# A decode layer on one Trainium2 core: other rows of w_down are loaded ahead, and on other queues

## The chip, the cores and the metric

The kernel runs on one core of a Trainium2 chip. The metric is the device time of one execution in microseconds. The kernel before has a median of 226.14 us over three runs (226.1 to 226.29).

## The reference

One token with 1024 features goes through an attention and a gated feed-forward layer side by side, and both are added to the token. Everything is float32.

```python
xn = _layernorm(x)
# attention: 32 query heads, 4 key/value heads of 128, the last W = 4096 rows of the cache
q = (xn @ wq).reshape(B, Sq, 32, 128).transpose(0, 2, 1, 3)
p = softmax(einsum("bhqd,bhkd->bhqk", q, k) * 128 ** -0.5)
A = einsum("bhqk,bhkd->bhqd", p, v)... @ wo          # 4096 -> 1024
# feed-forward: 1024 -> 3584 -> 1024
B = (gelu(xn @ w_gate) * (xn @ w_up)) @ w_down
return x + A + B
```

Every weight is used once, for one token. So each of the 94 MB of weights and cache rows is read from HBM once and used a single time.

## The kernel before, in words

All weights pass through one SBUF tensor, `ring`, with 32768 floats in each of 128 partitions. `PLAN` (lines 256 to 263) lists the loads in their order: what is loaded, to which place in the ring, and after the use of which earlier load. `used(key)` issues the loads that wait for `key`. Nearly all loads are issued by SyncE, on its queue. The order is wq, the first half of the keys and values, w_gate, the second half of keys and values, w_gate, w_up, wo, and last w_down in three groups of 16, 8 and 4 tiles, `("d", 0)` to `("d", 2)`. A tile of w_down is 128 rows by 1024 columns; row 4p + t of the last group's 512 rows is in partition p of its tile t.

Each weight is multiplied by a vector. TensorE does it for half of the tiles, as four matmuls that each write one of four partition groups of PSUM (`accumulate`, line 715); VectorE does it for the others by multiplying and adding into a partial sum (`add_scaled`), which TensorE adds up at the end (`units`). The results of the four column strips lie in partitions 31, 32, 95 and 96 (`ROW`). The token itself is loaded twice: as `x_rows` for the norm, and as `x_out` in these four partitions for the last sum.

`Flow` records every instruction's reads and writes, and in a second pass it gives each instruction the semaphore waits that it needs. An instruction waits in its engine's own order; what stands behind it on the same engine waits with it.

The last group, `("d", 2)`, has four tiles, 24 to 27. In the kernel before its first two tiles come in three loads (lines 319 to 325): all 2048 columns for the partitions 0, 2, 4, ..., all 2048 for 1, 5, 9, ..., and 1280 for 3, 7, 11, .... The other 768 columns of these 32 rows, which belong to tile 25, are loaded by `load_moved` (line 335), in ten small DMAs, nine of three rows and one of five. They are issued by SyncE between wo and w_down, as `("m", 0)` of the plan, and go to a tile of their own, `moved`. The last 768 columns of tile 25's place in the ring are cleared first by GpSimd (line 321), after wo's use of that part of the ring has ended, so that the 32 rows which don't come with these loads read as zero.

```python
nc.sync.dma_start(loaded[key][0:P:2, :2 * n], both[0:P:2])
nc.sync.dma_start(loaded[key][1:P:4, :2 * n], both[1:P:4])
nc.sync.dma_start(loaded[key][3:P:4, :end], both[3:P:4, :end])
```

The factors for these rows are picked out of the hidden vector by small matmuls and copies at the end of `hidden` (lines 685 to 698) into `moved_h`; `downs` (line 734) adds the moved rows on VectorE before it comes to the w_down tiles. All other factors of w_down lie in `hz`, one column for each tile.

After the first two tiles come tile 26, and tile 27 in three column pieces. The last sum takes the left half of tile 27 first, then the right half in two steps, and four stores end the kernel.

Of the kernel before, what the change touches and what calls it, by code (L numbers as in the profile page):

```python
# [5 lines left out]
F32 = mybir.dt.float32  # L6
# [5 lines left out]
P = 128  # L12
D = 1024
# [4 lines left out]
DF = 3584  # L18
NR = 4
NJ = D // (NR * P)  # L20
NB = 512
NA = DF // NB
CO = D // 4
TD = DF // P
WIDE = 16
DOWN = (16, 8, 4)
# [5 lines left out]
GELU_C = math.sqrt(2.0 / math.pi)  # L32

ROW = (31, 32, 95, 96)
MC = 768
MOVED = ((0, 0, 0, 12, 4), (0, 1, 12, 12, 4), (1, 0, 24, 5, 1), (1, 1, 29, 3, 1))
SIZES = {"tp": NB, "acc": 2 * NB, "part": 8 * NB, "rows": 2 * NB}


# [188 lines left out]
class Pool:  # L228
# [34 lines left out]
]  # L263

# [1 line left out]
def decode_layer(nc, x, k_cache, v_cache, wq, wo, w_gate, w_up, w_down, out):  # L266
    consts = stream = work = Pool(nc.nc, "sbuf")
# [11 lines left out]
    def grouped(w, start, rows):  # L279
        return w[start:start + P * rows, :].rearrange("(p t) n -> p t n", p=P)  # L280
# [17 lines left out]
    loaded = {}  # L298

    def load(key, at):  # L300
        kind, i = key
        if kind == "m":
            load_moved()
            return
        src = source(*key)
        if kind in "kv":

            loaded[key] = dst = ring[:, at:at + RING // 4]
            if kind == "v":
                nc.sync.dma_start(dst, src)  # L310
            else:
                for odd in range(2):
                    nc.sync.dma_start(dst[odd:P:2], src[:, odd])
            return
        rows, n = src.shape[1:]
        loaded[key] = ring[:, at:at + rows * n]
        dst = loaded[key].rearrange("p (t n) -> p t n", n=n)
        pieces = PIECES[i] if kind == "d" else (0, rows)
        if key == ("d", 2):
            end = 2 * n - MC  # L320
            nc.gpsimd.memset(loaded[key][:, end:2 * n], 0.0)
            both = src[:, 0:2].rearrange("p t n -> p (t n)")
            nc.sync.dma_start(loaded[key][0:P:2, :2 * n], both[0:P:2])
            nc.sync.dma_start(loaded[key][1:P:4, :2 * n], both[1:P:4])
            nc.sync.dma_start(loaded[key][3:P:4, :end], both[3:P:4, :end])
            pieces = pieces[1:]
        for t, end in zip(pieces, pieces[1:]):
            ends = (0, n // 2, 3 * n // 4, n) if key == ("d", 2) and end == rows else (0, n)
            for cols in (slice(*cut) for cut in zip(ends, ends[1:])):
                nc.sync.dma_start(dst[:, t:end, cols], src[:, t:end, cols])  # L330

    moved = consts.tile([P, 2, MC], F32, name="moved")
    moved_h = consts.tile([P, 2], F32, name="moved_h")

    def load_moved():


        rest = w_down[DF - 4 * P:, D - MC:].rearrange("(r x) n -> x r n", x=16)[13]
        for s, a, first, count, step in MOVED:
            for j in range(step):  # L340
                to = 32 * a + j
                nc.sync.dma_start(
                    moved[to:to + 4 * (count // step):4, s], rest[first + j:first + count:step]
                )

    def used(key):

        for new, at, old in PLAN:
            if old == key:
                load(new, at)  # L350
# [3 lines left out]
    x_in = x.rearrange("a b (j p) -> (a b j) p", j=NJ)  # L354
# [1 line left out]
        nc.scalar.dma_start(x_rows[j:j + 1, :], x_in[j:j + 1, :])  # L356
    x_out = work.tile([P, CO], F32, name="x_out")
    nc.vector.memset(x_out, 0.0)
    x_in = x.rearrange("a b (h c n) -> (a b c) h n", h=2, c=4)
    for c in (0, 2):  # L360
        nc.scalar.dma_start(
            x_out[ROW[c]:ROW[c] + 2, :].rearrange("c (h n) -> c h n", h=2), x_in[c:c + 2]
        )

    ident = consts.tile([P, P], F32, name="ident")
    nc.gpsimd.memset(ident, 0.0)
    nc.gpsimd.affine_select(
        out=ident, in_=ident, compare_op=ALU.not_equal, fill=1.0, base=0,
        pattern=[[-1, P]], channel_multiplier=1,
    )  # L370
    avg = consts.tile([P, P], F32, name="avg")
    nc.vector.memset(avg, 1.0 / D)

# [4 lines left out]

    hz = consts.tile([P, TD + 1, 32], F32, name="hz")
    nc.vector.memset(hz, 0.0)  # L380
    nc.gpsimd.memset(moved, 0.0)
    nc.gpsimd.memset(moved_h, 0.0)
    oz = consts.tile([P, HQ + 1, 32], F32, name="oz")
    nc.vector.memset(oz, 0.0)
    units = consts.tile([P, 2, 32], F32, name="units")
# [62 lines left out]
    def add_scaled(total, w, factor, first):  # L448

        if first:  # L450
            nc.vector.tensor_scalar(total, w, factor, None, op0=ALU.mult)
        else:
            nc.vector.scalar_tensor_tensor(total, w, factor, total, op0=ALU.mult, op1=ALU.add)
# [210 lines left out]
    def hidden():  # L664

        h_p = small("h_p")
        kept = ((0, 16, 0, 4), (1, 8, 0, 2), (1, 4, 2, 1))
        t = at = 0  # L670
        for b, count, c, n in kept:
            k = rows[b]
            m = NB // count
            flat = copies[b][:k].rearrange("p a n -> p (a n)")
            for i in range(count):
                nc.tensor.matmul(
                    h_p[:, at + i:at + n * count:count], flat[:, i:P * count:count],
                    ident[:k, 32 * c:32 * (c + n):32], start=True, stop=True,
                )
            for own in range(n):  # L680
                r = slice(m * own, m * own + m)
                cols = slice(at + count * own, at + count * own + count)
                nc.vector.tensor_copy(hz[r, t:t + count, 31], h_p[r, cols])
            t, at = t + count, at + n * count
        k = rows[1]
        flat = copies[1][:k, 0]
        spans = []
        for s, a, first, count, step in MOVED:
            start = 16 * first + 13
            taken = flat[:, start:min(start + 80 * step, NB):4 * step]  # L690
            n = taken.shape[1]
            nc.tensor.matmul(
                h_p[32 * a:32 * a + n, at + s:at + s + 1], taken, ident[:k, 64:65],
                start=True, stop=True,
            )
            spans.append((slice(32 * a, 32 * a + n), s))
        for r, s in spans:
            nc.vector.tensor_copy(moved_h[r, s:s + 1], h_p[r, at + s:at + s + 1])


    out_p = psum.tile([P, CO], F32, name="out_p", tag="out")
# [10 lines left out]
        stores.append(len(nc.ops))  # L712
        queue.dma_start(dst[c:c + 2], rows[ROW[c]:ROW[c] + 2, :])

    def accumulate(p, z, t, w, start, stop):
        w = w.rearrange("p (h c n) -> p c h n", c=4, n=CO // 2)
        z = z.rearrange("p t m -> p (t m)")
        for c in range(4):
            at = 32 * (t + c) + 31 - ROW[c]
            nc.tensor.matmul(  # L720
                p[32 * c:32 * c + 32], z[:, at:at + 32], w[:, c], start=start, stop=stop
            )

    def outputs(i):
# [9 lines left out]
    def downs():  # L734

        tiles = [loaded["d", i][:, n * D:(n + 1) * D] for i in range(3) for n in range(DOWN[i])]
        for s in range(2):
            add_scaled(out_part[:52, D - MC:], moved[:52, s], moved_h[:52, s:s + 1], False)
        for t in KEPT:
            add_scaled(out_part, tiles[t], hz[:, t, 31:32], False)  # L740
        order = [t for t in range(DOWN[0]) if t not in KEPT]
        half = DOWN[0] + DOWN[1] // 2
        for t in [*order[:6], *range(DOWN[0], half), *order[6:], *range(half, TD - 4)]:
            accumulate(out_p, hz, t, tiles[t], False, False)
        accumulate(out_p, units, 0, out_part, False, False)
        for t in range(TD - 4, TD - 1):
            accumulate(out_p, hz, t, tiles[t], False, t == TD - 2)

        n = CO // 2
        t, wt = TD - 1, tiles[TD - 1]  # L750
        nc.vector.tensor_add(y, out_p, x_out)
        first_p = small("first_p")[:, :n]
        accumulate(first_p, hz, t, wt[:, :NB], True, True)
        nc.vector.tensor_add(y[:, :n], y[:, :n], first_p)
        store(0, 0, y[:, :n])
        store(0, 2, y[:, :n])
        last_p = psum.tile([P, 2, NB], F32, name="last_p", tag="acc")
        z = hz.rearrange("p t m -> p (t m)")
        for c in (0, 2):
            r = slice(32 * c, 32 * c + 64)  # L760
            for k in (c, c + 1):
                at = 32 * (t + k) + 31 - ROW[k]
                nc.tensor.matmul(
                    last_p[32 * k:32 * k + 32, c // 2, :n], z[:, at:at + 32],
                    wt[:, NB + n * k:NB + n * k + n], start=True, stop=True,
                )
            nc.vector.tensor_add(y_last[r], y[r, n:], last_p[r, c // 2, :n])
            store(1, c, y_last)

    used(None)  # L770
    layer_norm()
    state = None
    half = RING // 8
# [77 lines left out]
```

## Time and profile before

| | before |
|---|---|
| time, median of three runs | 226.14 us |
| span of the profiled execution, first to last instruction | 224.8 us |
| SyncE's DMA queue (q1), share of the sixteen engines' span | 97.8% |
| moved over DMA, mean | 421 GB/s |
| TensorE busy / VectorE busy | 126.0 us / 112.1 us |
| GpSimd busy | 2.8 us |
| mean granted TensorE clock | 0.795 |

The profile describes one execution. Its time as a whole is not recorded beside the span; the span is 1.3 us below the median of the runs, and that difference lies before the first and after the last instruction. The share of a DMA queue is the time that its packets took, over the span of all sixteen DMA engines. Where the queue view is asked for a short stretch, it counts the packets that start in it, with their whole time, so a share can be over 100%. The chain of waits goes back from the last instruction, at each step to what released it.

### The profile page before, as it was taken

The numbers are of one execution on the slowest core, as the hardware profiler recorded it, in microseconds if no ns is written. First come the engines' busy times: TensorE is split into PE (matmuls) and PEld (weight loads), VectorE is DVE, ScalarE is ACT, GpSimd is POOL, SyncE is SP. The second block draws the span as 40 slices with busy tenths as digits, with TensorE's granted clock in tenths as the row PEclk, the third lists the DMA queues.
The fourth block names the chain that finished last, engine by engine and source line by source line (L and its number), as shares of the span: only waits on it lengthen the run. The fifth ranks groups of instructions, "written<-read, shape, count | busy, mean of one in ns | idle before, by whom it ended". The sixth has DMA issues, their size and how long they took to land.

```text
span 224.8 us, 2511 instructions
## 1 busy us (share of the span) xinstructions
PE 126.0 (56%) x1107; PEld 65.6 (29%) x1107; DVE 112.1 (50%) x142; ACT 28.2 (13%) x54; POOL 2.8 (1%) x9
## 2 busy tenths in 40 slices
PE   0120910539899891999836751237308988900976
PEld 0010200104634731755601110001003887400442
DVE  7030920591333282336039489339708932992942
ACT  2030000002415600454400220000000000000000
POOL 3000000000000000000000000000000000010000
PEclk9999975596969999799988795557965855665699
DMA  9889889799997999999989999999989989999994
GB/s 374 374 385 548 373 373 560 338 408 464 439 490 338 429 443 452 391 488 408 472 355 449 434 449 429 490 399 420 469 385 455 467 385 461 434 397 394 426 407 172
DMA packets 3194, 94.53 MB, mean 421 GB/s; under 512 B 446, under 2 KB 718, under 8 KB 1040
## 3 DMA queue, kind: packets, MB, share of 16 engines
q1 hardware_dynamic: 3160, 94.38, 97.8%
q8 instruction: 8, 0.13, 0.2%
q14 instruction: 2, 0.02, 0.0%
q10 hardware_dynamic: 24, 0.01, 0.0%
HBM read 94.38 MB, written 0.00 MB: 420 GB/s over the span
## 4 chain that ended last, share of the span: by engine, by line
DMA 67%; DVE 20%; PE 10%; SPq 1%; ACT 1%; issue 1%; POOL 0%; DVEq 0%
DMA ring<-in_B_w_gate 26%; DMA ring<-in_A_wq 18%; DMA ring<-in_A_wo 13%; DVE part L225 13%; DMA ring<-in_B_w_down 10%; PE tp L225 6%; PE out L225 3%; DVE out_part L225 3%; DVE rows L225 2%; SPq L225 1%; PE acc L225 1%; DVE g_sb L225 1%; ACT kT L225 1%; DVE hz L225 1%; DVE kT L225 0%
## 5 line engine op out<-in xcount | busy, mean ns | idle before, releaser
L225 PE MATMUL acc<-ring,xz 128*32 128x512 f32 x176 | 32.2, 808 | 37.3 <-DMA ring<-in_A_wq 22.2
L225 DVE SCALAR_TENSOR_TENSOR part<-ring,xz,part 128x3584 f32<-128x3584 f32 (+1 forms) x9 | 37.2, 4129 | 22.0 <-DMA ring<-in_A_wq 12.5
L225 PE MATMUL tp<-ident,ring 128*128 128x128 f32 x128 | 21.0, 309 | 7.1 <-DMA ring<-in_A_k_cache 5.0
L225 PEld LDWEIGHTS acc<-ring,xz 128*32 128x32 f32 x176 | 7.2, 139 | 58.2 <-issue 26.7
L225 DVE SCALAR_TENSOR_TENSOR out_part<-ring,oz,out_part 128x1024 f32<-128x1024 f32 x16 | 20.6, 1285 | 0.6
L225 PEld LDWEIGHTS tp<-ident,ring 128*128 128x128 f32 x128 | 15.4, 154 | 16.7 <-DMA ring<-in_A_k_cache 5.9
L225 PE MATMUL out<-ring,hz 128*32 128x256 f32 x168 | 12.1, 438 | 13.5 <-DMA ring<-in_B_w_down 13.4
L225 DVE COPY kT<-tp 128x512 f32<-128x512 f32 x12 | 8.1, 690 | 19.1 <-PE tp L225 19.1
L225 PE MATMUL out<-ring,oz 128*32 128x256 f32 x120 | 12.0, 586 | 9.6 <-DMA ring<-in_A_wo 9.6
L225 ACT ACTIVATE kT<-tp 128x512 f32<-128x512 f32 x20 | 11.5, 596 | 26.6 <-PE tp L225 26.6
L225 PE MATMUL tp<-ident,kT 128*128 128x4 f32 (+4 forms) x64 | 13.4, 343 | 1.6 <-DVE hz L225 1.6
L225 PEld LDWEIGHTS tp<-ident,kT 128*128 128x128 f32 (+2 forms) x64 | 13.1, 294 | 2.2 <-DVE hz L225 1.8
L225 PE MATMUL acc<-part,units 128*32 128x512 f32 x44 | 8.1, 817 | 8.7 <-DVE part L225 8.7
L225 DVE TENSOR_SCALAR part<-ring,xz 128x3584 f32<-128x3584 f32 (+1 forms) x3 | 6.5, 2171 | 12.3 <-DMA ring<-in_A_wq 7.5
L225 PEld LDWEIGHTS out<-ring,hz 128*32 128x32 f32 x168 | 5.6, 125 | 20.0 <-DMA ring<-in_B_w_down 15.8
L225 PEld LDWEIGHTS out<-ring,oz 128*32 128x32 f32 x120 | 5.7, 166 | 16.0 <-DMA ring<-in_A_wo 10.6
L225 DVE SCALAR_TENSOR_TENSOR out_part<-ring,hz,out_part 128x1024 f32<-128x1024 f32 x6 | 7.7, 1285 | 4.9 <-DMA ring<-in_B_w_down 4.7
L225 PE MATMUL s<-kT,qz 128*32 128x512 f32 x64 | 9.3, 709 | 0.0
L225 DVE TENSOR_REDUCE m<-s 128x2 f32<-128x1024 f32 x4 | 4.9, 1225 | 7.7 <-PE s L225 7.7
L225 PE MATMUL o<-ring,pT 128*32 128x128 f32 x256 | 7.8, 274 | 1.0 <-ACT pT L225 1.0
L225 PEld LDWEIGHTS o<-ring,pT 128*32 128x32 f32 x256 | 6.7, 110 | 1.9 <-ACT pT L225 1.9
L225 PE MATMUL tp<-ident,x_rows 2*128 2x2 f32 x4 | 0.6, 253 | 10.4 <-DMA x_rows<-in_A_x 10.4
(96 smaller groups left out, 73.3 us busy)
## 6 DMA issues: line engine op xcount, KB each, us to landing
ring<-in_B_w_gate SPq DMA_DIRECT2D x2, 7168.0 KB, 29.5
ring<-in_A_k_cache SPq DMA_DIRECT2D x4, 2048.0 KB, 19.0
ring<-in_A_v_cache SPq DMA_DIRECT2D x2, 4096.0 KB, 26.1
ring<-in_B_w_up SPq DMA_DIRECT2D x2, 3584.0 KB, 22.3
ring<-in_B_w_up SPq DMA_DIRECT2D x1, 7168.0 KB, 25.8
ring<-in_B_w_down SPq DMA_DIRECT2D x2, 2048.0 KB, 20.7
ring<-in_B_w_down SPq DMA_DIRECT2D x2, 512.0 KB, 21.1
ring<-in_B_w_down SPq DMA_DIRECT2D x2, 256.0 KB, 21.2
```

What stands on the lines that cost most here:

```text
L225: return lambda *a, **k: self.flow.issue(self.engine, lambda: call(*a, **k))
```

## The change

Instead of 768 columns of 32 rows, 256 columns (768 to 1023) of all 128 rows of the two tiles 24 and 25 are loaded ahead. The last group's first two tiles then come in one load of 768 columns each. The early rows are loaded at the start of the kernel. SyncE issues 51 of them (76 to 126) in one DMA and row 127 in another, right behind the two loads of wq. GpSimd issues the rows 0 to 75 in five DMAs of 17, 2, 34, 6 and 17 rows, and before them the two loads of `x_out`, which ScalarE issued. The `moved` tile has rows of 260 floats, of which 256 are used, so that the two tiles' pieces of a row stay two pieces.

The factors of these rows are those of `hz` anyway, so the small matmuls and copies into `moved_h` go. GpSimd no longer clears `moved`, `moved_h` and the part of the ring. TensorE leaves out the columns loaded ahead: in tiles 24 and 25 the strips 2 and 3 take their left half alone (`short` in `accumulate`). VectorE adds the early rows as 128 x 256 where it added 52 x 768.

```diff
-MC = 768
-MOVED = ((0, 0, 0, 12, 4), (0, 1, 12, 12, 4), (1, 0, 24, 5, 1), (1, 1, 29, 3, 1))
+MC = 256
+MOVED = 24
...
-    (("o", 0), 0, ("ub", 0)), (("o", 1), 16384, ("u", 1)), (("m", 0), None, ("u", 1)),
+    (("o", 0), 0, ("ub", 0)), (("o", 1), 16384, ("u", 1)),
...
         if key == ("d", 2):
-            end = 2 * n - MC
-            nc.gpsimd.memset(loaded[key][:, end:2 * n], 0.0)
-            both = src[:, 0:2].rearrange("p t n -> p (t n)")
-            nc.sync.dma_start(loaded[key][0:P:2, :2 * n], both[0:P:2])
-            nc.sync.dma_start(loaded[key][1:P:4, :2 * n], both[1:P:4])
-            nc.sync.dma_start(loaded[key][3:P:4, :end], both[3:P:4, :end])
+            nc.sync.dma_start(dst[:, 0:2, :n - MC], src[:, 0:2, :n - MC])
             pieces = pieces[1:]
...
-    moved = consts.tile([P, 2, MC], F32, name="moved")
-    moved_h = consts.tile([P, 2], F32, name="moved_h")
...
+    moved = consts.tile([P, 2, MC + 4], F32, name="moved")[:, :, :MC]
+
+    def load_moved(queue, first, count):
+        rows = grouped(w_down, P * MOVED, DOWN[2])[first:first + count, 0:2, D - MC:]
+        queue.dma_start(moved[first:first + count], rows)
...
-        nc.scalar.dma_start(
+        nc.gpsimd.dma_start(
             x_out[ROW[c]:ROW[c] + 2, :].rearrange("c (h n) -> c h n", h=2), x_in[c:c + 2]
         )
+    at = 0
+    for count in (17, 2, 34, 6, 17):
+        load_moved(nc.gpsimd, at, count)
+        at += count
...
-    nc.gpsimd.memset(moved, 0.0)
-    nc.gpsimd.memset(moved_h, 0.0)
...
+            n = 1 if t in short and c >= 2 else w.shape[2]
             nc.tensor.matmul(
-                p[32 * c:32 * c + 32], z[:, at:at + 32], w[:, c], start=start, stop=stop
+                p[32 * c:32 * c + 32, :n * CO // 2], z[:, at:at + 32], w[:, c, :n], start=start, stop=stop
             )
...
-            add_scaled(out_part[:52, D - MC:], moved[:52, s], moved_h[:52, s:s + 1], False)
+            add_scaled(out_part[:, D - MC:], moved[:, s], hz[:, MOVED + s, 31:32], False)
...
     used(None)
+    load_moved(nc.sync, 76, 51)
+    load_moved(nc.sync, 127, 1)
     layer_norm()
```

More of the change, by code (lines that the diff above doesn't have):

```diff
@@ L301, in load @@
         kind, i = key
-        if kind == "m":
-            load_moved()
-            return
         src = source(*key)
@@ L330, in load @@
                 nc.sync.dma_start(dst[:, t:end, cols], src[:, t:end, cols])
-    moved = consts.tile([P, 2, MC], F32, name="moved")
-    moved_h = consts.tile([P, 2], F32, name="moved_h")
[L335 to L344, printed above, removed]
+    moved = consts.tile([P, 2, MC + 4], F32, name="moved")[:, :, :MC]
+    def load_moved(queue, first, count):
+        rows = grouped(w_down, P * MOVED, DOWN[2])[first:first + count, 0:2, D - MC:]
+        queue.dma_start(moved[first:first + count], rows)
     def used(key):
@@ L358, in decode_layer @@
     nc.vector.memset(x_out, 0.0)
-    x_in = x.rearrange("a b (h c n) -> (a b c) h n", h=2, c=4)
-    for c in (0, 2):
-        nc.scalar.dma_start(
-            x_out[ROW[c]:ROW[c] + 2, :].rearrange("c (h n) -> c h n", h=2), x_in[c:c + 2]
-        )
     ident = consts.tile([P, P], F32, name="ident")
@@ L370, in decode_layer @@
     )
+    x_in = x.rearrange("a b (h c n) -> (a b c) h n", h=2, c=4)
+    for c in (0, 2):
+        nc.gpsimd.dma_start(
+            x_out[ROW[c]:ROW[c] + 2, :].rearrange("c (h n) -> c h n", h=2), x_in[c:c + 2]
+        )
+    at = 0
+    for count in (17, 2, 34, 6, 17):
+        load_moved(nc.gpsimd, at, count)
+        at += count
     avg = consts.tile([P, P], F32, name="avg")
@@ L684, in hidden @@
             t, at = t + count, at + n * count
[L685 to L698, printed above, removed]
     out_p = psum.tile([P, CO], F32, name="out_p", tag="out")
@@ L713, in store, with accumulate @@
         queue.dma_start(dst[c:c + 2], rows[ROW[c]:ROW[c] + 2, :])
-    def accumulate(p, z, t, w, start, stop):
+    def accumulate(p, z, t, w, start, stop, short=()):
         w = w.rearrange("p (h c n) -> p c h n", c=4, n=CO // 2)
@@ L746, in downs @@
         for t in range(TD - 4, TD - 1):
-            accumulate(out_p, hz, t, tiles[t], False, t == TD - 2)
+            accumulate(out_p, hz, t, tiles[t], False, t == TD - 2, (MOVED, MOVED + 1))
         n = CO // 2
```

## The prediction

> **What bounds the kernel now.** I read the page first (queues, then the chain of waits), then the windows over the last microseconds, then the queue view over stretches so short that they hold packets of one size.
>
> ```profile
> span 224.8 us, 2511 instructions
> ...
> DMA  9889889799997999999989999999989989999994
> ...
> q1 hardware_dynamic: 3160, 94.38, 97.8%
> q8 instruction: 8, 0.13, 0.2%
> q14 instruction: 2, 0.02, 0.0%
> q10 hardware_dynamic: 24, 0.01, 0.0%
> ...
> DMA 67%; DVE 20%; PE 10%; SPq 1%; ACT 1%; issue 1%; POOL 0%; DVEq 0%
> ```
>
> SyncE's queue (q1) alone keeps the sixteen DMA engines busy for 97.8% of the span: the kernel is a stream of 94 MB. The rest is start and tail. So an edit moves the time only if it changes when the last of the sixteen engines is through with its own share. The windows of the end show that they are not through together:
>
> ```profile
> core 0: us, PE busy (x) PEld busy (x) DVE busy (x) ACT busy (x) POOL busy (x), PEclk, DMA share, GB/s
> ...
> 200.00:219.00 19.00, 9.48 (x132) 4.72 (x136) 11.10 (x10) 0.00 (x0) 0.00 (x0) 0.68 0.96 408
> ...
> 220.00:220.50 0.50, 0.50 (x13) 0.16 (x9) 0.00 (x0) 0.00 (x0) 0.00 (x0) 1.00 1.01 385
> 220.50:221.00 0.50, 0.50 (x16) 0.26 (x8) 0.00 (x0) 0.00 (x0) 0.00 (x0) 1.00 0.75 287
> 221.00:221.50 0.50, 0.32 (x8) 0.00 (x0) 0.00 (x0) 0.00 (x0) 0.00 (x0) 1.00 0.77 281
> 221.50:222.00 0.50, 0.47 (x8) 0.16 (x8) 0.00 (x0) 0.00 (x0) 0.00 (x0) 1.00 0.69 240
> 222.00:222.40 0.40, 0.40 (x12) 0.16 (x8) 0.16 (x1) 0.00 (x0) 0.00 (x0) 1.00 0.17 56
> 222.40:223.00 0.60, 0.60 (x16) 0.29 (x8) 0.50 (x3) 0.00 (x0) 0.00 (x0) 1.00 0.00 0
> ```
>
> The next to last column is the busy share of the engines. It falls from 1.01 to 0.75 at about 220.5 and stays there for a microsecond: four of sixteen are done (I call them the leading four). The other twelve end between 221.5 and 222.4. Behind the last byte comes a tail that no part of the change touches:
>
> ```profile
> 200.11 21.38 DMA ring<-in_B_w_down
> ...
> 221.53 0.68 PE out L225 x8
> ...
> 222.24 0.43 DVE y L225
> ...
> 223.31 0.29 DVE y_last L225
> ```
>
> The next to last w_down tile lands at 221.49, and PE, the sum and the store follow. The last landing ends the kernel, whichever engine brings it.
>
> **Prices.** Six queue views over stretches of 36 to 700 ns, in this order: 221.70 to 222.40, 187.00 to 187.20, 216.50 to 216.56, 218.965 to 219.001, 162.6 to 162.7, 7.30 to 7.36. The share is the packets' time over sixteen times the stretch.
>
> ```profile
> DMA packets 98, 0.08 MB, mean 119 GB/s; under 512 B 17, under 2 KB 98, under 8 KB 98
> q1 hardware_dynamic: 98, 0.08, 34.6%
> ...
> DMA packets 8, 0.01 MB, mean 62 GB/s; under 512 B 4, under 2 KB 4, under 8 KB 8
> q1 hardware_dynamic: 8, 0.01, 16.2%
> ...
> q1 hardware_dynamic: 1, 0.01, 32.7%
> ...
> q1 hardware_dynamic: 3, 0.02, 121.7%
> ...
> q8 instruction: 1, 0.02, 68.7%
> ...
> q10 hardware_dynamic: 1, 0.00, 8.8%
> ```
>
> First row: 0.346 x 16 x 0.70 = 3.88 us for 81 packets of 1 KB (the last two column pieces of the last tile) and 17 completion marks. The second: 0.162 x 16 x 0.20 = 0.52 us for four packets of 3 KB (the old moved rows) and four marks. A straight line in size through both, with a mark at about 9 ns, gives **0.046 us for 1 KB and 0.121 us for 3 KB**. Third: 0.327 x 16 x 0.06 = **0.31 us for 8 KB**. Fourth: 1.217 x 16 x 0.036 = 0.70 us for one of 8 KB and two of 5 KB, so **0.195 us for 5 KB**. Fifth: an instruction fetch of 16 KB takes 0.687 x 16 x 0.1 = **1.10 us** of one engine. Sixth: ScalarE's queue pays 0.088 x 16 x 0.06 = 0.084 us for a 2 KB packet, which is what the line gives (0.046 + 0.037): a packet of another queue was no dearer there.
>
> The fetches explain the end. Eight of 1.1 us and one table on q14 make up to nine engines late, and the ten old moved DMAs cost three engines 10 x (0.121 + 0.009) = 1.30 us each. Nine and three are the twelve, and the lead of the four (220.5 against 221.5 to 222.4) is of that size. I read from it that the three engines of the moved rows are not among the nine; no row names an engine.
>
> **The change part by part**, engine by engine; 128 rows are eight per engine.
>
> *The late load of two tiles, all sixteen.* Before: six packets of 8 KB, two of 5 KB and three marks: 6 x 0.31 + 2 x 0.195 + 0.03 = 2.28 us. After: sixteen packets of 3 KB and one mark: 1.95 us. **-0.33 us on every engine.**
>
> *The early rows.* 256 columns of a row in two tiles are two packets of 1 KB, 0.092 us. A share of 17 rows is 17 x 0.092 = 1.56 us. Of 51 rows in one DMA I take three shares of 17, as the old moved DMAs were cut in three rows. GpSimd's 17, 34 and 17 make four more such shares, its 2 and 6 rows eight shares of one row, and one engine has none. Seven GpSimd DMAs leave marks, between none on an engine and 7 x 0.009 = 0.06 us; I take 0.06.
>
> The sum, by kind of engine:
> - the three of the old moved rows, if the 51 rows go there: -0.33 - 1.30 + 1.57 + 0.05 (the single row) + 0.06 = **about +0.05**;
> - eight of the nine with a fetch: -0.33 + 0.09 + 0.06 = **-0.18**; the ninth has no new row: -0.27 (and one old moved row less, or not);
> - the leading four, if GpSimd's shares of 17 fall on them: -0.33 + 1.56 + 0.06 = **+1.29**, so they end near 221.8.
>
> All but the first kind then end earlier than 222.4. Whether the very last engine is one of the nine (-0.2) or of the three (0) the rows do not tell. I take -0.19, nine of twelve being of the first sort; with marks and the single row left out it would be -0.3.
>
> Where GpSimd's shares fall is the unknown term; the rows bound it by the leading four (ending 221.8, not last) and by the last of the twelve (222.4 - 0.33 + 1.62 = 223.7, +1.3 us). I take the leading four because there are four such shares and four such engines, and because the three old shares can be seen to miss the fetches.
>
> [...]
>
> *What I cost at nothing, and what hides it.*
>
> ```profile
> 51.00 28.54 DMA ring<-in_B_w_gate
> ...
> 26.43 1.17 SPq L225 DMA_DIRECT2D ring<-in_A_k_cache  x2
> ...
> 71.07 1.12 SPq L225 DMA_DIRECT2D ring<-in_A_k_cache  x2
> ...
> 158.27 7.14 SPq L225 DMA_DIRECT2D moved<-in_B_w_down  x10
> ...
> 201.45 2.06 DVE L225 SCALAR_TENSOR_TENSOR out_part<-moved,moved_h,out_part 52x768 f32<-52x768 f32 x2
> ...
> DVE out_part L225 <- DMA ring<-in_B_w_down: 4.7, 1, 4.7
> 197.51 0.75 POOL ring L225
> q10 hardware_dynamic: 12, 0.01, 0.1%
> ```
>
> SyncE's two early DMAs stand behind wq's and before the k issue at 26.43, which is 25 us later, so nothing is held up in issuing; in the engines' order they come after wq, so the first k tile lands up to 1.6 us later on three engines. What is late next is the SyncE issue that waits for it, at 71.07, while w_gate runs until 79.54 (51.00 + 28.54): 8 us of cover. Without it the 1.6 us would show in full. Ten old issues (7.1 us of SyncE, 158 to 165) go; the w_down issue behind them was not due yet. GpSimd's memset of the ring (0.75 us at 197.5) held back loads that run some 20 us later; nothing. GpSimd waits for one more thing, VectorE's zeroing of x's tile in the first microseconds; behind it stand only its five loads. Its issue time is in no row; bounds are ScalarE's and SyncE's (7.14 / 10 = 0.71 each), 5 us for seven, and ten times that would still be early for 201.45. The packets take their turn between 64 KB packets: ScalarE's 12 packets on two engines needed 13 us (7 to 20 us, last row), 2.2 us each, so 34 need some 75 us, again well before 201. ScalarE loses two issues, next needed at 13 us. VectorE's two adds shrink from 768 to 256 columns and the small products and copies for the old rows go (some 3 us); VectorE then idles 4.7 us for w_down anyway. PE's eight half-width blocks lie in front of a wait for the next tile. x is needed at 222.24.
>
> **The rivals.**
> *A share on a late engine (slower).* One of GpSimd's 17-row shares falls on one of the twelve. For it speaks that no row shows a GpSimd DMA; against it the count of four and four. Its engine goes up by 1.29 instead of 0.15 or so: from 221.5 to 222.4 it ends at 222.8 to 223.7, a middle of 223.3, **+0.9 us: 227.0**. It decides as soon as that engine stood later than 221.1. The other place for it is a fetch that now falls on an engine with 17 rows: same size.
> *Rows spread evenly.* GpSimd cuts each DMA over all engines: 76 rows are 4.75 per engine, 0.44 us; -0.33 + 0.44 + 0.06 = **+0.15: 226.3**, within the bound. [...]
> *GpSimd's packets are dearer (slower).* The fetch is the row for it: 1.10 us for 16 KB, where twice 0.31 would be 0.62, so 1.8 times. Then 34 x 0.046 x 1.8 = 2.8 us, and the leading four end at 220.5 - 0.33 + 2.8 + 0.06 = 223.0: **+0.6 us: 226.7**. The 2 KB packet of ScalarE's queue speaks against it. It decides from 1.5 times on.
> *More than counted (faster).* Every late engine gains the full 0.33 and a fetch of the last one falls away or behind the stream, since PE has fewer instructions: **about -0.6: 225.5**. All fetches have to go right for it; the one at 216 us would move by a microsecond at most and stay inside.
>
> **How the numbers follow.** The three runs have a median of 226.14, the profiled execution a span of 224.8; 1.3 us lie around it and stay. The sum is -0.19 on the span, carried over to the median: **225.95 us**, its own range 225.8 to 226.2. Chances: forecast 0.56, share on a late engine 0.17, even spread 0.06, dearer packets 0.09, more than counted 0.12. About 0.2% (0.45 us) is what a measurement here can tell from no change. Faster: 0.12. Within: 0.56 and 0.06 make 0.62. Slower: 0.17 + 0.09 = 0.26. The range runs from 225.65, which leaves out most of the last case, to 227.0, which holds the dearer packets and half of the late share.
>
> **What would show it.** Right: the busy share has no step at 0.75 before the end, falls from about 221.5 and reaches zero some 0.2 us sooner; a new GpSimd queue with some 150 packets of 1 KB at 0.046 us; eight fetches as before. Wrong: the share stays at a few sixteenths after 222.4 (a share on a late engine, or dear packets, told apart by the price of one), or the last load of two tiles takes no less than before.

## The result

The changed kernel is slower: 229.26 us median (229.12 to 229.63, four runs) beside 226.13 us for the kernel before in the same comparison (226.1 to 226.29). The ratio is 1.0139, with a 95% interval of 1.0124 to 1.0153. That is +3.1 us, where the prediction had -0.19 and a range that ended at 227.0.

The page of the changed kernel, its first line, its queues and the shares of the chain of waits:

```profile
span 228.3 us, 2480 instructions
...
q1 hardware_dynamic: 3301, 94.22, 97.5%
q0 software_dynamic: 608, 0.17, 0.4%
q8 instruction: 8, 0.13, 0.2%
...
DMA 81%; DVE 16%; PE 2%; issue 0%; SPq 0%; DVEq 0%
```

SyncE's queue moves 0.16 MB less than before, which should take 0.4 us less of each engine (0.16 MB over 420 GB/s). But 97.5% of 228.3 us are 222.6 us, where 97.8% of 224.8 us were 219.9: its packets kept the engines busy for 2.7 us more. So the loss is not idle time. GpSimd's packets (q0) took 0.4% of the span, 0.9 us per engine, and the bytes that left SyncE's queue make up for about half of that. The rest is that the other packets became slower.

The windows say when. The kernel before, with the columns of the prediction (share of the DMA engines and GB/s last):

```profile
22.00:41.00 19.00, 6.25 (x32) 1.59 (x32) 6.83 (x2) 0.00 (x0) 0.00 (x0) 0.75 0.93 404
41.00:46.00 5.00, 4.08 (x24) 1.03 (x28) 4.03 (x1) 0.00 (x0) 0.00 (x0) 0.60 1.00 433
46.00:52.00 6.00, 2.05 (x24) 0.47 (x20) 4.94 (x2) 0.00 (x0) 0.00 (x0) 0.99 1.01 437
52.00:68.00 16.00, 15.10 (x92) 8.43 (x84) 4.13 (x9) 5.40 (x9) 0.00 (x0) 0.79 1.05 452
68.00:180.00 112.00, 68.58 (x643) 34.97 (x642) 61.94 (x66) 19.80 (x42) 0.00 (x0) 0.81 1.00 433
```

The changed kernel in the same windows:

```profile
22.00:41.00 19.00, 5.03 (x32) 1.30 (x32) 6.84 (x2) 0.00 (x0) 0.00 (x0) 0.79 1.03 436
41.00:46.00 5.00, 1.53 (x8) 0.40 (x12) 1.48 (x1) 0.00 (x0) 0.00 (x0) 0.50 1.01 295
46.00:52.00 6.00, 4.84 (x28) 0.96 (x20) 5.96 (x2) 0.00 (x0) 0.00 (x0) 0.66 0.94 373
52.00:68.00 16.00, 12.64 (x88) 7.22 (x88) 4.68 (x7) 3.97 (x7) 0.00 (x0) 0.89 1.03 422
68.00:180.00 112.00, 68.38 (x640) 33.27 (x637) 59.21 (x67) 21.05 (x44) 0.00 (x0) 0.77 1.01 433
```

A window counts the packets that start in it, so bytes and share swing together; GB/s over share is the rate of busy engines. Before, it is 434, 433, 433 and 430 GB/s up to 68 us. After, it is 423, **292**, 397 and 410. A stretch times the missing part gives the time lost: 19 x (1 - 423/434) = 0.5, 5 x (1 - 292/433) = 1.6, 6 x 0.083 = 0.5 and 16 x 0.047 = 0.7 us, together 3.3 us. From 68 us on both move 433 GB/s. The engines are busy throughout, and slow. 41 to 46 us is where SyncE's 51 rows are on their way, behind wq; GpSimd's rows are under way from 17 to 67 us.

The chain of waits of the changed kernel agrees:

```profile
53.55 30.03 DMA ring<-in_B_w_gate
...
89.71 30.27 DMA ring<-in_B_w_gate
...
197.90 23.86 DMA ring<-in_B_w_down
221.80 3.84 PE out L225 x60
```

The first w_gate lands at 83.58 us (79.54 before), 4.0 us late, and the second at 119.98, where the chain before had this row, which ends at 116.08:

```profile
85.66 30.42 DMA ring<-in_B_w_gate
```

So the lateness is there by 84 us and does not grow.

The end itself looks as it was meant to. The windows of the changed kernel's last microseconds:

```profile
224.00:224.50 0.50, 0.50 (x18) 0.42 (x12) 0.00 (x0) 0.00 (x0) 0.00 (x0) 1.00 0.99 356
224.50:225.00 0.50, 0.50 (x8) 0.03 (x2) 0.00 (x0) 0.00 (x0) 0.00 (x0) 1.00 0.86 293
225.00:225.50 0.50, 0.50 (x10) 0.16 (x8) 0.00 (x0) 0.00 (x0) 0.00 (x0) 1.00 0.28 96
225.50:226.00 0.50, 0.47 (x14) 0.18 (x10) 0.29 (x1) 0.00 (x0) 0.00 (x0) 1.00 0.04 14
```

There is no step at 0.75 any more: the engines end nearly together. At 224.0 to 224.5 us the share is still 0.99, where in the kernel before the last engine was done at 222.4: all sixteen are late.

### The profile page after: what moved, and what is told of

Its sections match the earlier page's. It is cut to its first block, busy times and chain, and to the rows that moved or that the text cites. A ratio compares the mean times of both kernels' runs of the same rounds, so it can differ in the third digit from the quotient of the medians.

```text
span 228.3 us, 2480 instructions
## 1 busy us (share of the span) xinstructions
PE 124.6 (55%) x1099; PEld 64.6 (28%) x1099; DVE 110.5 (48%) x138; ACT 28.0 (12%) x54; POOL 6.0 (3%) x13
## 3 DMA queue, kind: packets, MB, share of 16 engines
q1 hardware_dynamic: 3301, 94.22, 97.5%
## 4 chain that ended last, share of the span: by engine, by line
DMA 81%; DVE 16%; PE 2%; issue 0%; SPq 0%; DVEq 0%
DMA ring<-in_B_w_gate 26%; DMA ring<-in_A_wq 19%; DVE part L225 14%; DMA ring<-in_A_wo 13%; DMA ring<-in_B_w_up 11%; DMA ring<-in_B_w_down 10%; DVE out_part L225 2%; PE out L225 2%; PE acc L225 0%; PE tp L225 0%; SPq L225 0%; DVE y_last L225 0%; DVE d L225 0%; DVEq L99 0%
## 5 line engine op out<-in xcount | busy, mean ns | idle before, releaser
L225 PE MATMUL acc<-ring,xz 128*32 128x512 f32 x176 | 34.9, 892 | 44.3 <-DMA ring<-in_A_wq 25.6
L225 PE MATMUL tp<-ident,ring 128*128 128x128 f32 x128 | 20.0, 306 | 7.3 <-DMA ring<-in_A_k_cache 4.4
L225 PE MATMUL out<-ring,hz 128*32 128x256 f32 (+1 forms) x168 | 12.4, 450 | 14.6 <-DMA ring<-in_B_w_down 14.6
L225 PE MATMUL out<-ring,oz 128*32 128x256 f32 x120 | 10.4, 521 | 9.8 <-DMA ring<-in_A_wo 9.8
L225 PE MATMUL tp<-ident,kT 128*128 128x4 f32 (+2 forms) x56 | 13.1, 366 | 1.3 <-DVE hz L225 1.3
L225 PEld LDWEIGHTS tp<-ident,kT 128*128 128x128 f32 (+1 forms) x56 | 12.8, 319 | 1.9 <-DVE hz L225 1.5
L225 PE MATMUL acc<-part,units 128*32 128x512 f32 x44 | 7.4, 757 | 6.1 <-DVE part L225 6.1
L225 PEld LDWEIGHTS out<-ring,oz 128*32 128x32 f32 x120 | 4.7, 149 | 15.5 <-DMA ring<-in_A_wo 10.8
L225 PE MATMUL s<-kT,qz 128*32 128x512 f32 x64 | 7.7, 598 | 0.0
```

The source lines that it names most:

```text
L225: return lambda *a, **k: self.flow.issue(self.engine, lambda: call(*a, **k))
```

## The experiments

Each ran beside the kernel before, on the same chip. The ratio is to it, with its 95% interval. Between the chips the kernel before moved by less than 0.1 us (226.13 to 226.22), so that rows can also be compared with each other.

| kernel | median us | before us | ratio |
|---|---|---|---|
| changed kernel | 229.26 | 226.13 | 1.0139 [1.0124, 1.0153] |
| SyncE's 51 + 1 rows late | 229.24 | 226.22 | 1.0137 [1.0122, 1.0152] |
| GpSimd's 76 rows on SyncE, late | 229.17 | 226.22 | 1.0133 [1.0097, 1.0169] |
| 128 rows in one DMA, late | 226.58 | 226.22 | 1.0016 [1.0006, 1.0025] |
| the same, x on GpSimd | 226.63 | 226.22 | 1.0017 [1.0008, 1.0027] |
| 24 more rows, own partitions | 228.01 | 226.15 | 1.0074 [1.0056, 1.0091] |
| 24 more rows, 64 higher | 228.00 | 226.15 | 1.0087 [1.0068, 1.0107] |
| 24 more rows, 16 higher | 228.66 | 226.18 | 1.0106 [1.0086, 1.0127] |
| 128 rows in one DMA on GpSimd | 226.75 | 226.15 | 1.0023 [1.0013, 1.0033] |
| 64 + 64 rows on GpSimd | 227.78 | 226.18 | 1.0080 [1.0057, 1.0103] |
| 64 + 64 rows on SyncE, late | 227.82 | 226.18 | 1.0073 [1.0058, 1.0088] |
| 4 x 32 rows on SyncE, late | 227.93 | 226.18 | 1.0080 [1.0063, 1.0096] |
| before, all 32 moved rows 64 higher | 227.49 | 226.15 | 1.0056 [1.0039, 1.0073] |
| before, 8 moved rows 64 higher | 226.40 | 226.19 | 1.0009 [1.0000, 1.0019] |
| before, 3 moved rows 64 higher | 226.38 | 226.19 | 1.0004 [0.9995, 1.0013] |
| GpSimd's five DMAs beside 128 rows | 228.81 | 226.19 | 1.0115 [1.0100, 1.0131] |

### Undoing one half at a time

Theory G: GpSimd's queue slows SyncE's packets. Theory S: the 51 early rows at the seam between wq and the keys do it. "Late" is behind wo, where the old moved rows stood.

```diff
-    load_moved(nc.sync, 76, 51)
-    load_moved(nc.sync, 127, 1)
+    # the same two calls for ("m", 0), behind wo
```

> SyncE's 51 rows and single row are issued behind wo instead of behind wq; GpSimd's DMAs stay at the start. Theory G (SyncE's packets are slowed as long as GpSimd's queue has work, 2 to 70 us): the loss stays, 228.5 to 229.3 us, and the big packets between 42 and 52 us stay some tenths of a us too long. Theory S (the 51 early rows in 1 KB pieces at the seam between wq and the keys hold up all engines there): about 226.5 us, and the packets between 42 and 52 us have their normal time.

```diff
-    for count in (17, 2, 34, 6, 17): load_moved(nc.gpsimd, at, count)
+    # for ("m", 0): load_moved(nc.sync, 0, 64); load_moved(nc.sync, 64, 12); x on nc.scalar
```

> [...] Theory G: the loss goes, 226.0 to 226.6 us, no long packets at 42 to 52 us. Theory S: the part of the loss between 42 and 52 us stays, about 1.7 of 3.1 us, so 227.8 us or more.

```diff
-    # all early loads, on both queues
+    # for ("m", 0): load_moved(nc.sync, 0, 128); x on nc.scalar
```

> All 128 rows come in one DMA on SyncE's queue behind wo, x on ScalarE's queue: eight rows on each engine, nothing early. Both theories: no long packets; the sum is -0.33 us for the late load and +0.74 for eight early rows on every engine, +0.4 in all, 226.5 us, less 1.3 on the three engines of the old rows.

The fourth differs from the third in the queue of x alone.

```diff
-        nc.scalar.dma_start(x_out[...], x_in[c:c + 2])
+        nc.gpsimd.dma_start(x_out[...], x_in[c:c + 2])
```

> As the kernel without GpSimd DMAs (128 rows in one DMA behind wo), but x for the sum on GpSimd's queue: what the queue itself costs, without rows. Theory G with a cost by the time that the queue has work: done by some 16 us, so +0.1 to +0.3 us beside that kernel. Theory S: no difference.

Both halves kept the whole loss (229.24 and 229.17), and without either it was gone (226.58). Neither theory gives that. A third, S and G together, would want the halves to add up. The windows show more. SyncE's rows late, then GpSimd's rows on SyncE late, then 128 rows in one DMA late, each from 185 to 192 us:

```profile
185.00:192.00 7.00, 5.99 (x24) 5.82 (x24) 0.51 (x3) 0.00 (x0) 0.00 (x0) 0.50 1.13 408
```

```profile
185.00:192.00 7.00, 5.38 (x23) 5.20 (x22) 0.51 (x3) 0.00 (x0) 0.00 (x0) 0.50 1.05 378
```

```profile
185.00:192.00 7.00, 6.55 (x42) 5.20 (x45) 2.61 (x5) 0.00 (x0) 0.00 (x0) 0.50 0.96 403
```

Busy rates are 361, 360 and 420 GB/s. The rows that I had put late made a new slow stretch there, 7 x (1 - 361/420) = 1.0 us, and only the DMA of 128 rows made none. That pointed away from time, queue and bytes, and to the shape of the DMA. x for the sum on GpSimd's queue costs nothing that can be told (226.63 beside 226.58). The third kernel also tests the ledger of the prediction: +0.4 expected, +0.36 measured, with an interval from 0.1 to 0.6.

### Which partitions an engine writes

Theory P, a guess: in the large loads, each DMA engine writes partitions of its own; an engine that writes partitions of another one holds up the stream. By P the old moved rows (partitions 0 to 11 and 32 to 48, in steps of four), which were cheap, with 431 GB/s of busy rate at 185 to 192 us where the stream has 433, would all be in their engines' own partitions, and rows next to each other, 51 or 64 in a DMA, would not. No row here names an engine, so no run shows which partitions an engine writes; "own" below means places like those of the old moved rows. Theory H was that reads of 1 KB from few engines hold up HBM.

The pair for it takes the kernel with 128 rows in one DMA and adds 24 unused rows behind wq, of 4 KB in 1 KB pieces: eight DMAs of three rows, 98 KB, which I took to go to three engines. The two differ in one number, `a`, and a third run has it at 16, in the same half of the 128 partitions:

```diff
+    for n in range(8):
+        to = a + 32 * (n // 4) + n % 4          # a = 0, or 64, or 16
+        rows = grouped(w_down, P * MOVED, DOWN[2])[3 * n:3 * n + 3, 0:4, D - MC:]
+        nc.sync.dma_start(extra[to:to + 12:4], rows)
```

> [...] Theory P (a DMA engine that writes partitions which another engine writes in the large loads holds up the stream): no long packets at 42 to 52 us, 226.5 to 226.9 us; the three engines take 8 x 4 x 0.046 = 1.5 us more, of which they have about 1.2 in hand. Theory H (reads of 1 KB at a pitch of 16 KB from few engines hold up HBM): long packets, +1 us, 227.6 us.

> [...] Theory P: the packets of all engines at 41 to 45 us are long as in the changed kernel, +1.0 to +1.3 us against the other, 227.6 to 228.0 us. Theory H: no difference between the two.

> [...] Theory P: all engines' packets long at 41 to 46 us, about as with 64 partitions. If only the other half of the partitions is dear: packets as in the first of the pair.

The times hardly differ (228.0, 228.0, 228.7); by them alone theory P had failed. The windows differ. First the kernel without the 24 rows, from 22 us on:

```profile
22.00:41.00 19.00, 6.09 (x32) 1.52 (x32) 6.84 (x2) 0.00 (x0) 0.00 (x0) 0.74 0.91 393
41.00:46.00 5.00, 3.96 (x24) 1.03 (x28) 3.91 (x1) 0.00 (x0) 0.00 (x0) 0.62 1.05 452
46.00:52.00 6.00, 1.89 (x20) 0.43 (x16) 5.06 (x2) 0.00 (x0) 0.00 (x0) 0.97 0.99 421
52.00:68.00 16.00, 14.75 (x83) 8.40 (x76) 3.65 (x7) 4.12 (x7) 0.00 (x0) 0.71 1.05 452
```

Now the 24 rows: own partitions (a = 0), then 64 higher, then 16 higher, all from 41 to 46 us:

```profile
41.00:46.00 5.00, 3.87 (x20) 0.99 (x24) 3.82 (x1) 0.00 (x0) 0.00 (x0) 0.50 1.03 426
```

```profile
41.00:46.00 5.00, 3.78 (x24) 1.01 (x28) 3.73 (x1) 0.00 (x0) 0.00 (x0) 0.61 1.02 315
```

```profile
41.00:46.00 5.00, 3.90 (x20) 0.97 (x24) 3.85 (x1) 0.00 (x0) 0.00 (x0) 0.50 1.01 321
```

The rates are 414, 309 and 318 GB/s, where the kernel without the 24 rows has 430. With own partitions (as P counts them) the stream hardly notices: 0.2 us. With others' partitions it loses 5 x (1 - 309/430) = 1.4 us. The first of the pair is late for another reason: by my estimate three engines carry its 98 KB, and I had expected their 1.5 us to be nearly covered by a lead of 1.2; the rows cost 1.3 to 1.4 us. The ends show the two kinds of lateness, own partitions first, then 64 higher:

```profile
223.00:224.00 1.00, 1.00 (x18) 0.27 (x10) 0.00 (x0) 0.00 (x0) 0.00 (x0) 1.00 0.09 33
```

```profile
223.00:224.00 1.00, 1.00 (x27) 0.59 (x16) 0.00 (x0) 0.00 (x0) 0.00 (x0) 1.00 0.64 235
```

A share of 0.09 is one or two engines of sixteen; 0.64 is ten. So in the first a few engines are late, in the second most of the stream. What P had forecast for the two times, 1.0 to 1.3 us between them, was not measured all the same: the medians are equal. Why the two kinds of lateness don't add up in the second stays open, and the pair supports P by its rates alone.

The cleaner test leaves bytes per engine alone. In the kernel before, the moved rows and their factors go 64 partitions higher:

```diff
-MOVED = ((0, 0, 0, 12, 4), (0, 1, 12, 12, 4), (1, 0, 24, 5, 1), (1, 1, 29, 3, 1))
+MOVED = ((0, 2, 0, 12, 4), (0, 3, 12, 12, 4), (1, 2, 24, 5, 1), (1, 3, 29, 3, 1))
```

> The kernel before, with its moved rows and their factors 64 partitions higher (64 to 75 and 96 to 112 instead of 0 to 11 and 32 to 48), ten DMAs of 3 KB rows as before. Theory P: long packets on all engines at 186 to 190 us, +0.7 to +1.2 us, 226.9 to 227.4 us. Theory H: as the kernel before, 226.2 us.

VectorE's addition of these rows then spans 116 partitions instead of 52. It cost 1.3 us: 227.49 beside 226.15, a little above the range. The kernel before, and then this one:

```profile
185.00:192.00 7.00, 6.30 (x45) 5.22 (x49) 2.22 (x8) 0.00 (x0) 0.00 (x0) 0.50 1.01 435
```

```profile
185.00:192.00 7.00, 5.28 (x41) 4.11 (x45) 2.94 (x9) 0.00 (x0) 0.00 (x0) 0.50 1.03 370
```

431 against 359 GB/s is 7 x 0.167 = 1.2 us. The single packets say it too. The queue view of the kernel before from 185.20 to 186.40 us, and then of this one from 185.20 to 186.62:

```profile
DMA packets 9, 0.52 MB, mean 437 GB/s; under 512 B 1, under 2 KB 1, under 8 KB 1
q1 hardware_dynamic: 9, 0.52, 100.9%
```

```profile
DMA packets 13, 0.66 MB, mean 462 GB/s; under 512 B 3, under 2 KB 3, under 8 KB 3
q1 hardware_dynamic: 13, 0.66, 153.8%
```

Eight packets of 64 KB take 1.009 x 16 x 1.20 / 8 = 2.42 us each before. Here ten take 1.538 x 16 x 1.42 / 10 = 3.49 us each, the few ns of the completion marks included. All ten start within 1.42 us, less than one of them lasts. Sixteen packets of 64 KB in 2.42 us are 433 GB/s, the rate of the whole stream, so an engine has one of them at a time, and the ten are on ten different engines: the loss is not confined to a few. DMAs, their shapes, bytes and source are the same; the destination partition makes the difference.

The runs also set a limit to P. The two key loads behind wq are DMAs of 64 partitions as well, every second one (`dst[odd:P:2]`). The kernel before from 43 to 45 us:

```profile
DMA packets 28, 0.92 MB, mean 459 GB/s; under 512 B 0, under 2 KB 0, under 8 KB 0
q1 hardware_dynamic: 28, 0.92, 106.1%
```

28 packets of 32 KB take 1.061 x 16 x 2 / 28 = 1.21 us each, half of what 64 KB take, so the key loads run at the full rate. Whether an engine writes its own partitions in them, no run shows. So a DMA over fewer than 128 partitions is not dear by itself. What is dear may be that more arrives at one group of partitions than at the others, rather than that an engine leaves its own; the runs here fit both, and none tells them apart.

### GpSimd's queue with whole and with halved DMAs

```diff
-    for count in (17, 2, 34, 6, 17):
+    for count in (128,):                        # and (64, 64); SyncE has no early rows
```

> The 128 early rows in one DMA on GpSimd's queue at the start, and x there too; SyncE has no early rows. [...] Theory P: no loss, 226.5 to 226.8 us, SyncE's big packets keep their normal time. Theory G (GpSimd's queue with rows in it is what slows SyncE's packets): long packets while it drains, 227.5 us or more.

> As the kernel with 128 early rows in one DMA on GpSimd's queue, but cut into two DMAs of 64 rows. [...] Theory P with the price seen so far (1.2 us on all engines for 92 KB in the old moved rows 64 partitions higher, 13 ns per KB): +1.7 us, 228.4 us. Theory that few engines or a queue are the cause: no difference, 226.75 us.

One DMA of 128 rows through GpSimd's queue costs 0.6 us against the kernel before, 0.4 of which the ledger explains. Two of 64 cost another 1.0, where 1.7 was expected; the 1.7 takes half of the rows, 131 KB, to be outside their engines' own partitions, which no run shows. From 16 to 29 us, whole, then halved:

```profile
16.00:29.00 13.00, 5.35 (x28) 1.61 (x32) 5.35 (x2) 0.00 (x0) 0.00 (x0) 1.00 0.99 423
```

```profile
16.00:29.00 13.00, 4.59 (x28) 1.43 (x32) 4.59 (x2) 0.00 (x0) 0.00 (x0) 1.00 1.06 413
```

427 against 390 GB/s is 13 x 0.087 = 1.1 us. Theory G falls: GpSimd's queue by itself is not the cause.

### What sets the price

On SyncE's queue the late 128 rows were cut in two and in four.

```diff
-    load_moved(nc.sync, 0, 128)
+    # (0, 64), (64, 64)  and  (0, 32), (32, 32), (64, 32), (96, 32)
```

> As the kernel without GpSimd DMAs and with 128 rows in one DMA behind wo, but cut into two DMAs of 64 rows: same bytes, queue, place and rows per engine. Theory P: 131 KB to partitions of other engines, +1.7 us, 228.2 us. Otherwise no difference, 226.6 us.

> [...] Theory P with a price by the byte: about twice the loss of two DMAs of 64 rows, +3.2 us, 229.8 us. If the price is by the DMA or by the moment and not by the byte: as with two DMAs.

Two halves: +1.2 us against one DMA (227.82 and 226.58), a loss as P said, though less than the 1.7 expected. Four quarters: +1.35, where a price by the byte was to give twice the loss of the halves; that twice as many bytes lie outside their engines' own partitions is part of the guess. The rows, in this order:

```profile
185.00:192.00 7.00, 5.80 (x39) 4.48 (x42) 2.77 (x5) 0.00 (x0) 0.00 (x0) 0.50 1.00 346
```

```profile
185.00:192.00 7.00, 6.55 (x39) 5.34 (x43) 2.30 (x5) 0.00 (x0) 0.00 (x0) 0.50 0.98 337
```

So 98 KB of rows 64 partitions higher (+1.3 us) and 262 KB in halves (+1.2) or in quarters (+1.35) cost much the same. To tell a price by the burst from one by the byte, two kernels move only a few of the old rows higher.

```diff
-MOVED = (..., (1, 0, 24, 5, 1), (1, 1, 29, 3, 1))
+MOVED = (..., (1, 2, 24, 5, 1), (1, 3, 29, 3, 1))   # 8 rows; 3 rows: the last entry alone
```

> The kernel before with only the last two of its ten moved DMAs (5 and 3 rows, 25 KB) 64 partitions higher, the other eight where they were. Price by the byte: 25/98 of 1.3 us, +0.3 us, 226.5 us. Price by the burst: about +1.2 us, 227.4 us.

> The kernel before with only the last of its ten moved DMAs (3 rows, 9 KB) 64 partitions higher. Price by the byte: +0.1 us, 226.3 us. Price by the burst: about +1.2 us, 227.4 us.

Eight rows: +0.2 us; three rows: +0.2 us as medians, by the ratio +0.1 and not to be told from nothing. The two can't be told apart, but both are near the price by the byte, and far from 1.2 us for any burst. What holds the price at 1.2 to 1.4 us from 98 KB on stays open.

### GpSimd's share of the loss

The five DMAs of the changed kernel at the start, to a tile that nothing uses, beside 128 rows in one DMA late, with x on GpSimd's queue:

```diff
+        nc.gpsimd.dma_start(extra[at:at + count], rows)     # 17, 2, 34, 6, 17
```

> [...] Theory P: the stream is a little slow from 22 to 68 us, some 1.5 to 2 us in all, 228.1 to 228.6 us, no deep stretch at 42 to 46 us. If GpSimd's rows are only dear beside SyncE's: 226.6 to 226.9 us.

228.81 us, a little above theory P's range, +2.2 against the kernel with the 128 rows alone. Its windows:

```profile
22.00:41.00 19.00, 5.33 (x32) 1.37 (x32) 6.84 (x2) 0.00 (x0) 0.00 (x0) 0.82 1.02 433
41.00:46.00 5.00, 1.47 (x8) 0.40 (x12) 1.42 (x1) 0.00 (x0) 0.00 (x0) 0.50 0.95 373
46.00:52.00 6.00, 3.68 (x28) 0.75 (x20) 5.96 (x2) 0.00 (x0) 0.00 (x0) 0.86 1.00 394
52.00:68.00 16.00, 13.70 (x80) 7.09 (x80) 4.01 (x6) 4.01 (x6) 0.00 (x0) 0.79 1.04 427
```

425, 393, 394 and 411 GB/s, against 432, 430, 425 and 430 in the kernel with 128 rows alone, are 0.3 + 0.4 + 0.4 + 0.7 = 1.8 us. The other 0.4 us is about what the 156 KB of these unused rows take at 420 GB/s. It is a shallow loss over 46 us, as long as GpSimd's rows are under way, and there is no deep stretch at 41 to 46 us. That this shallow loss, too, comes from the partitions is argued from the halved DMAs on the same queue; no run gives these five DMAs other partitions, and their many tiny packets (below) are a rival for part of it. The deep one belongs to SyncE's rows; the kernel that keeps those early and has no GpSimd DMA shows it alone:

```profile
41.00:46.00 5.00, 3.68 (x24) 1.03 (x28) 3.63 (x1) 0.00 (x0) 0.00 (x0) 0.59 1.10 382
```

347 GB/s, 5 x (1 - 347/430) = 1.0 us. GpSimd's 1.8 and SyncE's 1.0 make 2.8 of the 3.3 us that the windows of the changed kernel lose; where both overlap (292 GB/s) they cost 0.2 us more than the sum of 0.4 and 1.0.

## Why the prediction was wrong

**The step that failed** is the price of the early rows. I wrote "a share of 17 rows is 17 x 0.092 = 1.56 us" and put it on the engine that carries it, and on no other. What they cost their engine is one thing; that their arrival slows the packets of all sixteen engines is the other, and it is some 3 us. The destination is what matters in the runs that change it alone; that most of these 260 KB go to partitions of other engines is how theory P reads it, and no run shows it. The row that I took as nearest, the four 3 KB packets at 187 us, was cheap for a reason that I had not seen: the old moved rows had been placed in partitions 0, 4, 8 and so on, by P each in the partitions of the engine that carries it. The address pattern in `load_moved` said so (`moved[to:to + 4 * (count // step):4, s]`), and the factors were moved by matmuls and copies to fit it. I costed this as overhead that the change removes. Shown by: the kernel before with its rows 64 partitions higher, +1.3 us.

**None of the rivals was it.** The share on a late engine and the dearer packets both gave a few engines that end late (227.0 and 226.7). The end shows sixteen that end nearly together, so a late share is out; halved DMAs carry the same rows as whole ones, eight for each engine if they too use all sixteen, and still lose 1.0 to 1.2 us, so it is not a matter of a few engines. Rows spread evenly would have cost +0.15 us, and the faster case asked for a gain. The shares in GpSimd's DMAs that the sum assumes fit the packets on its queue: the trace of the changed kernel has 32 of 4 KB and 12 of 2 KB, which four shares of 17 rows and eight single rows make in packets of at most two rows (rows spread evenly would make 18 and 40). Which engines they are on no row shows, and that the 51 rows are three shares of 17 stays an assumption; what the runs showed in place of a late share is a slower stream, 292 to 423 GB/s of busy rate from 22 to 68 us where it had 430 to 434.

**What held.**
- The stream sets the end, and the step at 0.75 is gone. That the shares of 17 rows fell on the leading four would give this; no row names an engine, so it is not shown.
- The ledger of bytes by packet prices: 128 rows in one DMA were to cost +0.4 us and cost +0.36 (0.1 to 0.6).
- All that was costed at nothing, as far as the runs bear on it: x on GpSimd's queue (226.63 beside 226.58), and issue slack, since 4 us of lateness at the first w_gate did not grow later.
- Eight fetches, as before.

**What did not hold beside the main step**: "some 150 packets of 1 KB" on GpSimd's queue. There are 608. The queue view of the changed kernel from 28 to 40 us shows that nearly all are tiny (the first line counts all queues):

```profile
DMA packets 158, 5.19 MB, mean 433 GB/s; under 512 B 74, under 2 KB 74, under 8 KB 79
q1 hardware_dynamic: 79, 5.18, 101.0%
q0 software_dynamic: 79, 0.02, 0.7%
```

79 packets, of which 74 are under 512 B; the other five are of 4 KB. Together they took 0.007 x 16 x 12 = 1.34 us. At the prediction's prices, 0.158 us for 4 KB and 0.009 for a tiny one, they would take 1.46, so GpSimd's packets were not dearer. Their own time explains little of the loss.

## What to carry to other kernels

When a stream keeps all DMA engines busy, a small DMA beside it is not priced by its bytes alone: look at which partitions it writes. Cheap here were a DMA over all 128 partitions (+0.36 us), the address pattern in steps of four (431 GB/s of busy rate), and the key loads over every second partition (1.21 us for 32 KB); 64 + 64 adjacent rows in place of 128 cost 1.2 us. In the profile such a cost is not idle time: the busy share stays at 1.0 while GB/s falls (1.01 and 295 at 41 to 46 us of the changed kernel), so divide one by the other, window by window, before and after. And a layout that looks like needless work (the old rows' factors moved to odd partitions) can be the thing that makes a trick pay: ask what it is for before its removal is counted as a gain.

## What the runs showed of the hardware that I had not expected

- A few rows can slow the whole stream, by where they are written: 24 rows 64 or 16 partitions higher gave 309 and 318 GB/s of busy rate against 414, for some 5 us. With the old moved rows 64 partitions higher, packets on ten engines at once took 3.49 us in place of 2.42. Why the others suffer is open.
- The distance does not matter much: 16 partitions higher (318 GB/s) is as dear as 64 (309).
- The loss grows with the bytes at first (9 and 25 KB: 0.1 to 0.2 us; 98 KB: 1.3 us) and then stays (128 rows in two and in four DMAs: 1.2 and 1.35 us).
- With GpSimd's five DMAs beside 128 rows the rate is only 2 to 9% lower (425 against 432 GB/s to 393 against 430), but for the 46 us in which their rows are under way.
